# Row blocks 2 to 7 of w3 transposed on VectorE, in a Nystrom attention with a folded feed-forward

## Chip, core and metric

The kernel runs on one core of a Trainium2 chip. A core has five engines with queues of their own, each strictly in order: TensorE (PE, matrix products; PEld is its loading of weights), VectorE (DVE), ScalarE (ACT), GpSimd (POOL) and SyncE (SP), which here only issues transfers. They share an on-chip memory of 128 partitions (SBUF) and an accumulator memory (PSUM) that TensorE writes and VectorE and ScalarE read. 16 DMA engines move data between it and the chip's memory; transfers are issued on the queues of SP, ACT (together "hardware", q1 and q10 in the profile) and POOL ("software", q0, which can also change the type). The metric is the device time of one execution in microseconds (us), as the median of the runs shown.

## What is computed

Inputs: q, k, v of shape (8 batches, 8 heads, 576 rows, 64), and weights w1, w2 (512 x 1024), w3 (1024 x 1024), w_out (1024 x 512), all f32.

```python
q_lm = q.reshape(B, H, m, S // m, D).mean(axis=3)      # m = 32 landmarks, S = 576
k_lm = k.reshape(B, H, m, S // m, D).mean(axis=3)
A, Bm, C = sm(q, k_lm), sm(q_lm, k_lm), sm(q_lm, k)    # softmax of scaled products
Z = Bm^T / (norm1(Bm) * norminf(Bm) + 1e-6)
for _ in range(6):
    Z = 2 * Z - Z @ Bm @ Z
x = (A @ Z @ C @ v), heads side by side                # (4608, 512)
out = ((x @ w1) * (x @ w2)) @ w3 @ w_out               # (4608, 512)
```

## The kernel before

**Folding the weights.** w3 @ w_out doesn't depend on the data, so the kernel multiplies these two first, into `w34` (1024 x 512, f16 in SBUF). w3 is handled in eight row blocks j of 128 rows. A product on TensorE sums over partitions, so a row block has to be turned: its 1024 columns must lie along the partitions. `turn(j, cc)` (L514) does that for one half cc of 512 columns: four transposes of 128x128 on TensorE (L517) into a PSUM tile `big`, then a split of the result, scaled by 256, into two f16 parts, the high one by ScalarE (L522) and the rest by VectorE (L523); both are kept in `w3t`, four tiles of it. `split(c)` (L508) makes the same two parts of a block of 128 rows of w_out (L510, L511). `product(j, c)` (L526) adds three products of 128x512 (high x high, high x low, low x high; L530) into one PSUM tile; after c = 7 ScalarE writes the row block to `w34` (L533). In all 8 x 8 x 3 = 192 products and 16 turns.

**The loads.** w3 goes through three f32 buffers `w3f`, w_out through six `wof`. `load_w3` (L570) issues a row block as one transfer on SP of 128 rows of 4 KB (blocks 0 and 1 in two halves). q and k come through POOL's queue (L107), which changes them to f16, into two buffers `qkn`; the first of these transfers stands behind a copy on POOL (`gate`, L603) that waits until w_out's piece 4 has landed, so the first weights come ahead of q and k. `paced_w3` (L617) holds row block 4 back in the same way until batch 0's k is there.

**Attention.** For each batch VectorE transposes q and k in blocks of 32x32 (L143), landmarks are sums of rows (`landmarks`, L206 to L216; VectorE for batch 0, POOL for the others), `exchange` moves halves of them between partitions (L219; by TensorE for batches 0 and 1, by transfers for the others), then scores A, B, C (`scores_a`, `scores_b`, `scores_c`), the inverse (`norms`, `squares`, six steps of `inverse`), `values`, `denominators`, `normalise` and `landmark_values`.

**Feed-forward.** `project` (L430) makes, for a batch, g = (Z C v) w1 and the same with w2; `up(j, w)` (L451) multiplies A's normalised rows with g: four products of 288 columns each (L455), ScalarE copies the one for w1 (L459), VectorE multiplies it with the one for w2 (L461) into `ab`. `down(n, half)` (L470) multiplies 128 rows of `ab` with `w34` (L495), ScalarE copies the result (L499) and SP stores it (L502). 64 `up` pairs and 36 `down` of eight products.

**The order.** The text `ORDER` is the program's order: a list of words, each of which emits one step (F the next step of the fold, TK and TQ transposes of k and q, SK and SQ landmarks, E, B, C, A and so on, U for `up`, W for `down`). A word emits all its instructions on all engines at that place, so the queues of all engines follow one list. All of the fold's steps are emitted ahead of the first `up`, because `ab` takes the memory of the fold's pool (L668 to L673). Queues run ahead of one another as far as waits allow.

Of the kernel before, what the change touches and what calls it, by code (L numbers as in the profile page):

```python
# [29 lines left out]
CHAINS = ((0,), (1, 2), (3, 4), (5, 6), (7,))  # L30

ORDER = """
F F F F F F F F F F F F F TK0.0 F F F F F TQ0.0 TQ1.0 F F L3.3 F TK1.0 F F F F F SK0.0 SK1.0 F F
SQ0.0 P.4 F F F F L3.5 F L3.7 F F TQ0.1 TK0.1 SQ1.0 F F L3.6 TK1.1 F E.0 F B.0 F C0.0 SK0.1 N.0
F F F A0.0 R.0 FV.0 TQ1.1 F SK1.1 F I0.0 F F D.0 I1.0 F I2.0 Y0.0 Y1.0 SQ0.1 Y2.0 LK0.2 F X.0 F
I3.0 LK1.2 F F F I4.0 V0.0 V1.0 SQ1.1 LQ0.2 LQ1.2 E.1 F LK0.3 TK0.2 TK1.2 F LK1.3 I5.0 F V2.0
LV0.2 F TQ0.2 TQ1.2 A0.1 Z.0 SK0.2 LV0.1 LV1.1 F M0.0 LV2.1 F LV3.1 D.1 Y0.1 Y1.1 Y2.1 G0.0 G1.0
G2.0 M1.0 SK1.2 F SQ0.2 TK0.3 G3.0 TK1.3 C0.1 X.1 F F F F U0a.0 U0b.0 U1a.0 U1b.0 U2a.0 U2b.0
LQ0.3 TQ0.3 LQ1.3 LK0.4 U3a.0 LV1.2 V0.1 U3b.0 SQ1.2 E.2 U4a.0 U4b.0 B.1 U5a.0 U5b.0 N.1 V1.1
SK0.3 V2.1 R.1 U6a.0 U6b.0 TQ1.3 U7a.0 I0.1 M0.1 LK1.4 LQ0.4 U7b.0 W0.0 SK1.3 I1.1 W1.0 I2.1  # L40
A0.2 LV2.2 TK0.4 LV3.2 W0.1 I3.1 TK1.4 W1.1 I4.1 M1.1 LQ1.4 W0.2 TQ0.4 I5.1 W1.2 SQ0.3 SQ1.3
TQ1.4 Z.1 SK0.4 E.3 SK1.4 SQ0.4 LV0.3 C0.2 G0.1 D.2 G1.1 G2.1 W0.3 Y0.2 G3.1 V0.2 V1.2 Y1.2 V2.2
LV0.4 Y2.2 U0a.1 U0b.1 LV1.3 LK0.5 U1a.1 U1b.1 LV1.4 LK1.5 X.2 U2a.1 U2b.1 U3a.1 U3b.1 Z.2 SQ1.4
E.4 U4a.1 U4b.1 U5a.1 G0.2 TK0.5 U5b.1 U6a.1 U6b.1 M0.2 LQ0.5 LQ1.5 W1.3 U7a.1 LV2.3 U7b.1 LV3.3
M1.2 W0.4 G1.2 G2.2 G3.2 B.3 TK1.5 W1.4 U0a.2 A0.3 W0.5 U0b.2 U1a.2 LV2.4 D.3 Y0.3 Y1.3 SK0.5
U1b.2 Y2.3 C0.3 W1.5 LK0.6 U2a.2 U2b.2 U3a.2 W0.6 X.3 U3b.2 U4a.2 N.3 SK1.5 V0.3 V1.3 V2.3 R.3
U4b.2 TK0.6 W1.6 LV3.4 U5a.2 U5b.2 W0.7 TQ0.5 U6a.2 I0.3 M0.3 LK1.6 TQ1.5 W1.7 I1.3 SQ0.5 LQ0.6
U6b.2 W0.8 I2.3 W1.8 I3.3 U7a.2 U7b.2 W0.9 I4.3 M1.3 W1.9 I5.3 A0.4 LQ1.6 Z.3 C0.4 W0.10 G0.3
G1.3 G2.3 D.4 W1.10 Y0.4 LV0.5 SQ1.5 G3.3 E.5 LV1.5 U0a.3 U0b.3 Y1.4 W0.11 TK1.6 Y2.4 U1a.3
U1b.3 U2a.3 U2b.3 LK0.7 X.4 TK0.7 W1.11 TQ0.6 U3a.3 U3b.3 U4a.3 V0.4 V1.4 V2.4 SK0.6 SK1.6 A0.5  # L50
TQ1.6 W0.12 U4b.3 LV2.5 U5a.3 LV3.5 LK1.7 SQ0.6 U5b.3 Z.4 U6a.3 U6b.3 LV0.6 LV1.6 U7a.3 U7b.3
W1.12 M0.4 M1.4 G0.4 W0.13 SQ1.6 E.6 TK1.7 G1.4 G2.4 G3.4 SK0.7 W1.13 D.5 Y0.5 LQ0.7 Y1.5 Y2.5
C0.5 U0a.4 X.5 W0.14 SK1.7 W1.14 U0b.4 U1a.4 U1b.4 B.5 V0.5 V1.5 V2.5 U2a.4 U2b.4 N.5 W0.15
U3a.4 U3b.4 W1.15 A0.6 TQ0.7 R.5 M0.5 W0.16 U4a.4 I0.5 U4b.4 U5a.4 I1.5 U5b.4 U6a.4 I2.5 LV0.7
LQ1.7 TQ1.7 SQ0.7 SQ1.7 W1.16 I3.5 U6b.4 U7a.4 I4.5 M1.5 U7b.4 I5.5 LV2.6 LV1.7 LV3.6 W0.17 Z.5
C0.6 E.7 W1.17 D.6 G0.5 G1.5 G2.5 W0.18 Y0.6 Y1.6 G3.5 Y2.6 U0a.5 U0b.5 X.6 W1.18 U1a.5 U1b.5
U2a.5 B.7 V0.6 V1.6 V2.6 U2b.5 U3a.5 N.7 U3b.5 W0.19 U4a.5 U4b.5 U5a.5 U5b.5 Z.6 U6a.5 W1.19
LV2.7 G0.6 G1.6 G2.6 LV3.7 R.7 W0.20 A0.7 I0.7 W1.20 U6b.5 M0.6 M1.6 W0.21 U7a.5 G3.6 D.7 I1.7
U7b.5 W1.21 U0a.6 U0b.6 Y0.7 U1a.6 Y1.7 U1b.6 W0.22 W1.22 C0.7 U2a.6 W0.23 U2b.6 U3a.6 Y2.7
U3b.6 W1.23 V0.7 V1.7 V2.7 X.7 I2.7 U4a.6 W0.24 U4b.6 I3.7 U5a.6 W1.24 I4.7 U5b.6 U6a.6 I5.7  # L60
W0.25 Z.7 U6b.6 W1.25 M0.7 M1.7 G0.7 W0.26 U7a.6 U7b.6 W1.26 G1.7 G2.7 G3.7 W0.27 U0a.7 U0b.7
W1.27 U1a.7 U1b.7 W0.28 U2a.7 U2b.7 W1.28 U3a.7 U3b.7 U4a.7 W0.29 W1.29 U4b.7 U5a.7 U5b.7 W0.30
U6a.7 U6b.7 U7a.7 W1.30 U7b.7 W0.31 W1.31 W0.32 W1.32 W0.33 W1.33 W0.34 W1.34 W0.35 W1.35
# [4 lines left out]
def kernel(  # L68
# [93 lines left out]
    def constants():  # L162

        mask4 = consts.tile([128, 4, 32], FP32, name="mask4")
        eye = consts.tile([128, 2, 32], FP32, name="eye")
        onesq = consts.tile([128, 2, 4, 2, 4], FP16, name="onesq")
        nc.vector.memset(mask4, 0.0)
        nc.vector.memset(onesq, 0.0)
        for h in range(4):
            sl = slice(32 * h, 32 * h + 32)  # L170
            nc.vector.memset(mask4[sl, h, :], 1.0)
            for qd in range(2):
                nc.vector.tensor_copy(out=eye[sl, qd, :], in_=ident[sl, sl])
                nc.vector.memset(onesq[sl, qd, :, qd, h:h + 1], 1.0 / X64)

        selc = consts.tile([128, 2, 4, 128], FP16, name="selc")
        lomask = consts.tile([128, 1], FP32, name="lomask")
        selr = consts.tile([128, 8], FP32, name="selr")
        nc.vector.memset(selc, 0.0)
        nc.vector.tensor_tensor(out=selr, in0=eye[:, 0, 0:8], in1=eye[:, 0, 8:16], op=ALU.add)  # L180
        nc.vector.reduce_sum(out=lomask, in_=eye[:, 0, 8:16], axis=AX.X)
        nc.vector.tensor_scalar(out=lomask, in0=lomask, scalar1=-1.0, scalar2=None, op0=ALU.mult)
        for c in range(4):
            sl = slice(32 * c, 32 * c + 32)
            for qd in range(2):
                nc.vector.tensor_copy(
                    out=selc[sl, qd, c, :].rearrange("p (h m) -> p h m", m=32),
                    in_=selr[sl, 4 * qd:4 * qd + 4].unsqueeze(2).to_broadcast([32, 4, 32]),
                )
        eye2 = consts.tile([128, 32], FP32, name="eye2")  # L190
        nc.vector.tensor_tensor(out=eye2, in0=eye[:, 0], in1=eye[:, 0], op=ALU.add)
        bt = consts.tile([128, 4, 64], FP32, name="bt")
        for i in range(4):
            nc.vector.tensor_copy(out=bt[:, i, 32:64], in_=eye[:, 0])
        xsp = [consts.tile([128, 256], FP32, name=f"xsp{i}") for i in range(2)]
        for t in xsp:
            nc.vector.memset(t, 0.0)
        return mask4, eye, eye2, onesq, selc, lomask, bt, xsp


# [18 lines left out]
    def exchange(st):  # L219
        if st["b"] < 2:  # L220
            psE = big()
            for x in range(2):
                nc.tensor.matmul(psE[:, 0, 256 * x:256 * x + 256], pick[:, x, :],
                                 st["lm"][:, :, x].rearrange("p t l c e -> p t (l c e)"),
                                 start=True, stop=True)
            nc.scalar.copy(out=st["lm"].rearrange("p t x l c e -> p x t (l c e)"),
                           in_=psE[:, 0, :].rearrange("p (x t f) -> p x t f", x=2, t=2))
            return
# [104 lines left out]
    def values(st, n):  # L333
        if n == 0:
            st["psV"] = big()
# [169 lines left out]
    def fold(pf, wof, w3f, wsp, warm_up):  # L505
# [39 lines left out]
        for n, (j, c) in enumerate(order):  # L545
            for f, *args in before.get(n, ()):
                f(*args)
# [158 lines left out]
```

## Time and profile before

| what | value |
|---|---|
| median of 3 runs | 264.17 us (264.1 to 264.42) |
| span of the profiled execution, first to last instruction | 261.8 us |
| TensorE busy | 251.5 us, 96% |
| VectorE busy | 173.8 us, 66% |
| ScalarE busy | 134.7 us, 51% |
| GpSimd busy | 103.2 us, 39% |
| transposes of w3 on TensorE (L517) | 64, first at 4.6 us, last at 57.0 us |
| low halves of w3 on VectorE (L523) | 16, 687 ns each |
| DMA: bytes moved, mean rate | 37.78 MB, 144 GB/s |

One execution was recorded; its span is 2.4 us less than the median of the timed runs, which are other executions and have what lies around the span in them. In rows of the profile "line engine operation, out<-in xcount | busy us, mean ns of one | idle us before, what ended it" the tiles go by the program's names, and L517 is line 517 of the code above. TensorE's products overlap, so a row's mean duration is longer than the distance from one to the next.

### The profile page before, as it was taken

Reading aid. Unit: us, or ns where it says so; the run is one execution under the profiler, and the core shown is the slowest. Engines: PE = TensorE matmul, PEld = TensorE weight load, DVE = VectorE, ACT = ScalarE, POOL = GpSimd, SP = SyncE. Lnnn points to the kernel's source line nnn. Section 1 sums busy time; section 2 is a strip of 40 time slices with the busy share of each in tenths; the row PEclk is TensorE's granted clock in tenths of the full one; section 3 lists DMA queues with packets and bytes.
Section 4 is the critical chain, followed back from the end, with each engine's and each line's share of the span. In section 5 each row is a group of like instructions: output and inputs, shape, how many; then the busy total and the mean of one; then the engine's idle time right before and its main releaser. Section 6 shows DMA issues by size and latency. Waiting matters only on the chain.

```text
span 261.8 us, 10518 instructions
## 1 busy us (share of the span) xinstructions
PE 251.5 (96%) x4578; PEld 148.7 (57%) x4578; DVE 173.8 (66%) x352; ACT 134.7 (51%) x305; POOL 103.2 (39%) x134
## 2 busy tenths in 40 slices
PE   7999999998989999999999999999999999999993
PEld 3455554454556558557654674766476556656642
DVE  8765887556958687788856958767775656464410
ACT  4543236343652565576449546746646555455531
POOL 3630018998981999027092597504400000000000
PEclk9999999999999999999999999999999999999999
DMA  6999998999963448976668496933640713222355
GB/s 236 333 243 284 245 248 191 183 137 240 175 105 50 120 101 167 216 195 114 131 100 162 101 214 150 161 58 86 147 86 3 173 43 80 45 62 61 81 118 127
DMA packets 25070, 37.78 MB, mean 144 GB/s; under 512 B 4672, under 2 KB 13120, under 8 KB 25024
## 3 DMA queue, kind: packets, MB, share of 16 engines
q1 hardware_dynamic: 14704, 24.65, 36.9%
q0 software_dynamic: 9728, 11.54, 28.1%
q10 hardware_dynamic: 592, 0.92, 1.1%
q8 instruction: 36, 0.59, 1.0%
q14 instruction: 10, 0.08, 0.1%
HBM read 38.80 MB, written 9.44 MB: 184 GB/s over the span
## 4 chain that ended last, share of the span: by engine, by line
PE 89%; DVE 4%; ACT 3%; issue 1%; DMA 1%; SPq 0%; DVEq 0%; ACTq 0%
PE big L455 23%; PE acc L495 22%; PE acc L530 14%; PE big L442 5%; PE big L344 5%; PE big L399 4%; PE big L517 2%; PE small L530 2%; PE big L382 2%; PE small L421 2%; PE big L274 1%; PE big L495 1%; PE big L322 1%; DVE ab L461 1%; PE small L248 1%
## 5 line engine op out<-in xcount | busy, mean ns | idle before, releaser
L455 PE MATMUL big<-ahat,gt 128*128 128x288 f16 x512 | 73.1, 287 | 0.7 <-DVE ab L461 0.6
L495 PE MATMUL acc<-w,ab 128*128 128x512 f16 x264 | 67.2, 380 | 0.0
L461 DVE TENSOR_TENSOR ab<-a_sb,big 128x576 f16<-128x576 f16 x64 | 48.0, 750 | 27.2 <-ACT a_sb L459 16.8
L455 PEld LDWEIGHTS <-gt 128*128 128x128 f16 x512 | 48.3, 98 | 21.1 <-issue 3.1
L459 ACT CAST a_sb<-big 128x576 f16<-128x576 f32 x64 | 40.8, 640 | 33.9 <-PE big L455 32.9
L206 POOL TENSOR_TENSOR tr<-qkT 128x1024 f32<-128x1024 f16 x14 | 29.7, 2123 | 70.0 <-DVE qkT L143 69.8
L530 PE MATMUL acc<-wsp,w3t 128*128 128x512 f16 x168 | 41.3, 380 | 0.7 <-ACT w L533 0.5
L495 PEld LDWEIGHTS <-ab 128*128 128x128 f16 x280 | 25.3, 98 | 24.9 <-issue 3.5
L499 ACT ACTIVATE o_sb<-acc 128x512 f32<-128x512 f32 x33 | 19.8, 599 | 19.5 <-PE acc L495 19.1
L530 PEld LDWEIGHTS <-w3t 128*128 128x128 f16 x192 | 18.1, 98 | 18.9 <-issue 1.3
L143 DVE STREAM_TRANSPOSE qkT<-qkn 128x576 uint32<-128x576 uint32 x32 | 24.0, 763 | 2.0 <-DMA qkn<-in_k_dram 2.0
L448 DVE TENSOR_SCALAR gt<-big 128x1024 f16<-128x1024 f32 x16 | 19.1, 1211 | 3.1 <-PE big L442 3.0
L446 ACT ACTIVATE gt<-big 128x1024 f16<-128x1024 f32 x16 | 15.9, 1032 | 5.9 <-PE big L442 5.9
L211 POOL TENSOR_TENSOR tr<-tr 128x512 f32<-128x512 f32 x14 | 17.9, 1282 | 0.6
L442 PE MATMUL big<-wup,zt 64*32 64x512 f16 x512 | 17.4, 380 | 0.2 <-ACT en L282 0.2
L523 DVE SCALAR_TENSOR_TENSOR w3t<-big,w3t 128x512 f16<-128x512 f32 x16 | 11.0, 687 | 10.0 <-ACT w3t L522 10.0
L522 ACT ACTIVATE w3t<-big 128x512 f16<-128x512 f32 x16 | 9.5, 596 | 13.9 <-PE big L517 13.8
L284 DVE STREAM_TRANSPOSE ent<-en 128x576 f32<-128x576 f32 x16 | 12.1, 768 | 4.4 <-ACT en L282 4.4
L344 PE MATMUL big<-vt,ent 64*32 64x64 f32 x1152 | 14.2, 226 | 0.0
L282 ACT ACTIVATE en<-big 128x288 f32<-128x288 f32 x32 | 12.7, 411 | 2.9 <-PE big L274 2.7
L344 PEld LDWEIGHTS big<-vt,ent 64*32 64x32 f32 x1152 | 12.7, 105 | 2.0 <-ACT a_sb L459 0.5
L328 ACT ACTIVATE eat<-big 128x576 f16<-128x576 f32 x16 | 9.6, 652 | 7.3 <-PE big L322 7.3
(214 smaller groups left out, 285.2 us busy)
## 6 DMA issues: line engine op xcount, KB each, us to landing
out_dram<-o_sb SPq DMA_DIRECT2D x70, 128.0 KB, 2.5
vt<-in_v_dram SPq DMA_DIRECT2D x16, 288.0 KB, 5.3
vt<-in_v_dram SPq DMA_DIRECT2D x32, 144.0 KB, 4.0
qkn<-in_k_dram POOLq DMA_DIRECT2D x12, 288.0 KB, 5.4
qkn<-in_q_dram POOLq DMA_DIRECT2D x12, 288.0 KB, 4.9
w3f<-in_moe_w_dram SPq DMA_DIRECT2D x6, 512.0 KB, 6.7
wup<-in_moe_w_dram POOLq DMA_DIRECT2D x4, 512.0 KB, 25.3
wof<-in_moe_w_out_dram SPq DMA_DIRECT2D x6, 256.0 KB, 4.5
```

The lines of the kernel that those rows point to most:

```text
L143: nc.vector.transpose(out=st["qkT"][:, t, prs].rearrange("p c r q e -> p (c r q e)").bitcast(U32), in_=st["qkn"][:, t, prs, :].rearrange(" ...
L206: add(out=tr, in0=x[:, :, 0:4, :], in1=x[:, :, 4:8, :], op=ALU.add)
L211: add(out=tr[:, :, 0:2, :], in0=tr[:, :, 0:2, :], in1=tr[:, :, 2:4, :], op=ALU.add)
L344: nc.tensor.matmul(psV[32 * o:32 * o + 32, qd, 0:64], ent[sl, pr, r, :], vt[sl, pr, 64 * r:64 * r + 64], start=(r == 0), stop=(r == RT - 1 ...
L442: nc.tensor.matmul(psG[o:o + 32, qd, :], zt[rs, i, h, :], wup[rs, h, w, fs], start=(i == 0), stop=(i == 1), tile_position=(64 * qd, o))
L448: nc.vector.tensor_scalar(out=g[:, :, w, fs], in0=psG, scalar1=1.0 / ZS, scalar2=None, op0=ALU.mult)
L455: nc.tensor.matmul(p[:, c, 0:HS], st["g"][:, qd, w, 128 * j:128 * j + 128], st["ahat", qd][:, c, :], start=(qd == 0), stop=(qd == 1))
L459: nc.scalar.copy(out=st["a_sb"], in_=p[:, :, 0:HS])
L461: nc.vector.tensor_tensor(out=st["ab"][:, j, st["t0"]:st["t0"] + S].rearrange("p (c s) -> p c s", c=2), in0=st["a_sb"], in1=p[:, :, 0:HS], ...
L495: nc.tensor.matmul(pso[:, :], ab[:, j, t0:t0 + 128], w34[:, j, :], start=(j == 0), stop=(j == 7))
L499: nc.scalar.activation(out=o_sb, in_=pso, func=AXF.Copy, scale=1.0 / (X64 * X64))
L530: nc.tensor.matmul(psW[j][:, :], turned[j, c // 4][:, a, c % 4, :], wsp[:, b, c, :], start=(c == 0 and a + b == 0), stop=(c == 7 and a == 1))
```

## The change

Row blocks 0 and 1 of w3 are still turned by TensorE. Row blocks 2 to 7 are turned by VectorE's transpose, which turns each block of 32x32 by itself. To make that a whole turn, the row block is loaded with its four groups of 32 rows and 128 columns laid out so that only turns inside 32 partitions are left: partition 32a + r holds, for each of four row groups g, 128 neighbouring columns of row 32g + r. That takes eight transfers a row block, each of 32 x 4 pieces of 128 columns (512 B), in place of one. The transpose reads every fourth column; so the columns of w3 that lie along the partitions are taken in steps of four, and w_out's rows are loaded in the same steps, and so are the columns that TensorE's transposes read. The turned block goes to a tile `en`, which the scores C use too (two buffers in SBUF), and is split from there.

```diff
+NPE = 2
...
     def load_w3(j, cc=None, eng=nc.sync):
...
-        sl = slice(0, DF) if cc is None else slice(512 * cc, 512 * cc + 512)
-        eng.dma_start(out=w3f[j][:, sl], in_=moe_w3[128 * j:128 * (j + 1), sl])
+        src = moe_w3[128 * j:128 * j + 128, :]
+        if j < NPE:
+            sl = slice(0, DF) if cc is None else slice(512 * cc, 512 * cc + 512)
+            eng.dma_start(out=w3f[j][:, sl], in_=src[:, sl])
+        else:
+            for x in range(2):
+                for a in range(4):
+                    eng.dma_start(
+                        out=w3f[j][32 * a:32 * a + 32, 512 * x:512 * x + 512].rearrange("r (g f) -> r g f", g=4),
+                        in_=src.rearrange("(g r) (x a f) -> x a r g f", g=4, x=2, a=4)[x, a])
...
-        eng.dma_start(out=wof[c], in_=moe_w_out[128 * c:128 * c + 128, :])
+        eng.dma_start(out=wof[c], in_=moe_w_out.rearrange("(x m c) o -> x c m o", x=2, c=4)[c // 4, c % 4])
...
+    def turned_w3(j, cc):
+        if j < NPE:
+            wt = big()[:, 0, :]
+            src = w3f[j].rearrange("p (x m c) -> p x c m", x=2, c=4)
+            for c in range(4):
+                nc.tensor.transpose(out=wt[:, 128 * c:128 * c + 128], in_=src[:, cc, c], identity=ident[:, :])
+        else:
+            wt = pat.tile([128, 2, RT * 32], FP32, name="en").rearrange("p c f -> p (c f)")[:, 0:512]
+            src = w3f[j].rearrange("p (x g i c) -> p x c g i", x=2, g=4, c=4)
+            nc.vector.transpose(out=wt.rearrange("p (c g r) -> p c g r", c=4, g=4), in_=src[:, cc])
+        yield
+        w3t = w3ts[j, cc] = pf.tile([128, 2, 4, 128], FP16, name="w3t", bufs=4)
+        hi, lo = (w3t[:, i].rearrange("p c j -> p (c j)") for i in range(2))
+        nc.scalar.activation(out=hi, in_=wt, func=AXF.Copy, scale=WS)
+        yield
+        nc.vector.scalar_tensor_tensor(out=lo, in0=wt, scalar=WS, in1=hi,
+                                       op0=ALU.mult, op1=ALU.subtract)
```

The second part: every step becomes a generator that yields between its parts on different engines, and `ORDER` (now some 1,500 words) names a step once for each of its parts. So the parts of one step no longer stand together in the list: its part on VectorE can come behind other steps' parts for TensorE. `up` for instance:

```diff
-    def up(st, j, w):
-        p = big()
+    def up(st, j):
+        for w in range(2):
+            p = big()
...
+            yield
+            if w == 0:
+                a_sb = po.tile([128, 2, HS], FP16, name="a_sb", bufs=2)
+                nc.scalar.copy(out=a_sb, in_=p[:, :, 0:HS])
+                yield
+        nc.vector.tensor_tensor(...)
...
+    pab, live = [], {}
+    for word in ORDER.split():
+        if word not in live:
+            if word[0] == "U":
...
+            work = started(word)
+            if word == "K":
+                continue
+            live[word] = work
+        if live[word] is not None:
+            next(live[word], None)
```

In the new `ORDER` (S is `split`, Tx.j half x of row block j, F.j one step of row block j's product, KC the constants, LF the first loads behind the gate, LK and LQ loads of halves of k and q, L loads of w3):

```diff
+K K K KC KC T0.0 KC T0.0 T0.0 S.0 K S.0 K LO.6 K S.1 K K K KC K S.1 K T0.1 T0.1 LK1.2 T0.1 F.0 S.2
+S.2 F.0 LO.7 L.2 LK0.2 F.1 F.1 KC S.3 T1.0 S.3 KC L.3 T1.0 S.4 S.5 F.1 F.0 T1.1 T1.0 F.0 KC LF S.6
...
+TK1.0 F.2 F.2 T1.2 F.2 T0.3 P.4 T1.2 KC F.2 TK0.0 F.2 L.6 F.2 F.2 LQ1.2 F.2 T1.3 T0.3 F.1 TQ1.0 F.2
```

Both halves of batch 2's k (LK1.2, LK0.2) now stand ahead of LF, so POOL issues them before the gate; batch 2's q halves are issued between the first loads of batches 0 and 1. Batches 0 and 2 hold the two `qkn` buffers, so batch 1's k and q are loaded once batch 0's are transposed, and w1 and w2 behind them on POOL's queue (before: directly behind batch 0's and 1's loads). The row blocks are loaded in the order 2, 3, 4, 6, 5, 7 (before: 2, 3, 4, 5, 7, 6).

## The prediction

> **What bounds the kernel now.** I read the page first (busy shares, chain), then the table by stages, the groups of TensorE and VectorE, the chain around one turn, and the DMA view.
>
> ```profile
> PE 251.5 (96%) x4578; PEld 148.7 (57%) x4578; DVE 173.8 (66%) x352; ACT 134.7 (51%) x305; POOL 103.2 (39%) x134
> ...
> PE 89%; DVE 4%; ACT 3%; issue 1%; DMA 1%; SPq 0%; DVEq 0%; ACTq 0%
> ...
> 0.00:17.50 17.50, 15.79 (x72) 7.57 (x73) 12.45 (x54) 8.34 (x14) 8.51 (x24) 1.00 0.93 278
> 17.50:37.60 20.10, 19.60 (x106) 10.59 (x105) 15.16 (x26) 6.13 (x11) 0.18 (x1) 1.00 1.14 255
> 37.60:69.50 31.90, 30.32 (x611) 15.73 (x609) 20.55 (x45) 15.99 (x44) 28.02 (x33) 1.00 1.01 192
> 69.50:99.10 29.60, 27.63 (x820) 17.59 (x819) 22.40 (x44) 15.05 (x38) 22.50 (x26) 1.00 0.51 97
> 99.10:254.00 154.90, 154.56 (x2959) 95.08 (x2956) 102.83 (x186) 87.66 (x195) 44.02 (x52) 1.00 0.55 115
> ```
>
> The last five rows are stretches: length, then busy time of PE, PEld, DVE, ACT, POOL, granted clock (full everywhere), DMA share, GB/s. TensorE sets the end: from 99.1 us to its last product it is idle 0.3 us, in 69.5 to 99.1 2.0 us, before that 3.8 us (1.2 at the start, 1.3 one stall at 58.6 that nothing in the profile explains). 69.5 is where the first `up` product (L455) starts; all turning of w3 lies before it. So the change acts in the first 69.5 us, where the DMA engines are full as well (share 0.93 to 1.14) and VectorE has holes (21 us idle of 69.5).
>
> ```profile
> 22.95 0.44 PE big L517 x4
> 23.39 1.96 PE acc L530 x9
> ...
> 25.37 0.60 ACT w L533
> ...
> L517 PE MATMUL big<-ident,w3f 128*128 128x128 f32 x64 | 10.0, 280 | 0.3 <-DMA w3f<-in_moe_w_dram 0.3
> ...
> L523 DVE SCALAR_TENSOR_TENSOR w3t<-big,w3t 128x512 f16<-128x512 f32 x16 | 11.0, 687 | 10.0 <-ACT w3t L522 10.0
> ...
> L284 DVE STREAM_TRANSPOSE ent<-en 128x576 f32<-128x576 f32 x16 | 12.1, 768 | 4.4 <-ACT en L282 4.4
> ```
>
> The first three are pieces of the chain (start, length): a turn of four blocks holds the chain for 0.44 us though one transpose is shown as 280 ns, since they overlap. VectorE's 10.0 us of waiting ahead of L523 is for ScalarE's half of the split, which itself waits for the turn.
>
> **The change, part by part.**
>
> *TensorE loses 12 of 16 turns* (48 of 64 transposes; the built program's list has exactly 48 fewer): 12 x 0.44 = 5.3 us. Every other product is there in the same number, the 12 warm-up products too.
>
> *VectorE gains 12 transposes* of 128x512 f32. Rows: 768 ns for 576 columns (L284), 285 for 128 (L262), so 1.08 ns a column and about 0.70 us each: 8.4 us. The source is read with a stride of four elements; bound: L216, which also reads with a stride, takes 290 ns for 128 columns, and L355, which doesn't, 291. So nothing to 10% more; I take nothing. ScalarE and the second half read SBUF instead of PSUM: L510 and L511 do that in 622 and 676 ns against 596 and 687; no cost.
>
> Adding up every queue of the built program up to the first `up` product with these rows' durations (products by their spacing on the chain, 0.216 us for 512 columns): TensorE 62.3 us before, 57.0 after; VectorE (to its first L461) 54.5 before, 62.3 after; ScalarE 31 in both. VectorE becomes the longer queue of the front. Rows overlap a little (its 54.5 is about 49 of busy time), so it's about even with TensorE, and what decides is what it waits for, in order.
>
> *The loads of w3.* Each of six row blocks was one DMA of 128 packets of 4 KB (issue 0.33 us); it is now eight DMAs, 1024 packets of 512 B: 48 issues, 15.8 us on SP. SP is idle then, but each of its DMAs waits for the eighth one before it to land, so a block follows another only as that lands. Price of a packet:
>
> ```profile
> q1 hardware_dynamic: 430, 0.78, 103.5%
> ...
> q1 hardware_dynamic: 251, 0.90, 60.4%
> q0 software_dynamic: 309, 0.34, 49.2%
> ...
> q0 software_dynamic: 548, 0.61, 120.2%
> ```
>
> Queue, packets, MB, share of 16 engines: at 8 to 10 us alone, at 22 to 26 with POOL's queue q0, and q0 alone at 18 to 21. 2 KB packets take 77 ns (103.5% x 32 us / 430), 4 KB ones 154: no fixed part, so 512 B would be 22 ns. Bounds: 15 ns (the exchange at 70 to 73 us, 216 packets of about 190 B in 6.8% of 48 us) and 77 ns. I take 22, being on the line through both rows. With both queues full they take turns packet by packet (251 to 309). At one 22 ns packet to each of q0's (about 90 ns, 1.15 KB), w3 moves 73 KB/us, against 225 before (0.90 MB in 4 us).
>
> *POOL's queue.* Batch 2's k (0.59 MB) is now loaded ahead of the gate on wof[4], issued at 3.2 us where POOL's constants end; 2.7 us later (issue 9.5, first packets at 12.2 in this trace) it shares the engines with the first weights, and takes 2.9 us of them (0.205 MB/us). So wof[4] lands at 11.8 instead of 9.0, batch 0's q and k start at 15.0 instead of 12.2, and its q lands at about 22.5 (21.0). The first products need each wof piece at about that time; I count 1.3 us of stall to the end of blocks 0 and 1. The two turns that are gone there (0.9 us) hide most of it.
>
> *The chain through VectorE*, row by row: w3[2]'s first half lands at 15.2, right behind the wof pieces; from 15.0 on q0 is full, so its second half (0.26 MB at 73 KB/us) takes until 18.6 and w3[3]'s first until 22.2, landing at 22.6. VectorE's turn of w3[3] stands ahead of batch 0's first transpose and of the low half of w3[2], for which TensorE's fifth step of block 2 waits: TensorE stands there some 4 us. From 22.6 VectorE has 15.5 us of work (four turns, four low halves, four qkn transposes, landmarks 6.5 us) and 0.5 of waiting until batch 0's landmarks are done: 38.3. With bytes shared evenly it would be 36. Before, the exchange that needs them (L223) ran at 37.6, with three more product steps (1.9 us) and five turns still to come. From there TensorE needs 31.9 - 2.7 (five turns: 2 x 0.44, 3 x 0.59 on the chain) + 1.9 - 2.8 (its waits before) = 28.3 us, VectorE about 28, both in order and tied to one another (inverse, values, denominators): 2 us of waits on top. First `up`: 36 + 30.3 = 66.3 to 38.3 + 30.3 = 68.6, against 69.5; I take 67.5, the middle.
>
> *The order behind that* moves the same instructions: TensorE has 170.5 us by the same rows in both, VectorE and ScalarE the same. There is 2.3 us of idle time to win and nothing else; I take 0. The tail from the last product on (last copy waits for all stores) is unchanged.
>
> *Sum.* 261.8 - 2.0 = 259.8 for the span; the median of the runs is 264.17, 2.4 more than the profiled span, so 262.2.
>
> **The rivals.**
>
> Full gain: shares are kinder than packet by packet, VectorE is never late, TensorE keeps its idle 3.8 us: first `up` at 57.0 + 7.2 = 64.2 us; 264.17 - 5.3 = 258.9. For it: VectorE's 21 us of holes. Against: 8.4 us of turns and the q and k of batch 0 later by 1.5 us.
>
> Slower, by starved loads: packets of 512 B cost what 2 KB ones do (77 ns). w3 then moves 45 KB/us beside q0: w3[3]'s halves land at 27 and 32.5 instead of 22.6 and 26.1, everything on VectorE behind them is 6 us later, and the first `up` comes at 67.5 + 6 = 73.5: 264.17 + 4.0 = 268.2. It decides from about 35 ns a packet (2 us, by the same proportion). Or, with cheap packets, if a queue's turn is several of them: the counts of 251 to 309 fit turns of any equal length, but a new DMA holds only 8 packets for each engine (128 over 16; 0.18 us), and against 12 of q0's, say (1.1 us), 64 KB come in 1.28 us, 50 KB/us, nearly the same rate and the same time. For both: full engines, queues in order. Against: the straight line through two sizes, and that no row shows turns of many. [...]
>
> Slower or same, by the new order: TensorE was idle 0.3 us after 99.1, so each hole of the new order is a loss: 0.5 to 1 us of waits in each of the four pairs of batches takes the 2.0 back and up to 2 more, 264 to 266. For it: nothing of the old slack is in reserve; against: products of two `up` steps are interleaved, and between scores and norms of batches 1 and 2 now stand 4.7 us of other products where TensorE had waited 1.0 us.
>
> That the turns stay is excluded by the built list.
>
> **How the numbers follow.** Forecast 45% (260.5 to 264.3; its upper end is no change), full gain 14%, starved loads 28% (16 by dear packets, 12 by long turns), new order 13%. 0.2% (0.5 us) is about what a measurement of this kernel tells from no change. Faster: 40 + 14 = 54%; same: 5 of the forecast, 5 of the order = 10%; slower: 28 + 8 = 36%. Range 258.3 to 267.5: it leaves out the worse half of the starved loads and a little below.
>
> **What would show it.** First `up` at 66 to 69 us; TensorE with a wait of some 4 us for a low half of w3t near 21 us and one of 1 to 3 us at the exchange; VectorE's transposes 0.70 us; w3 packets 22 ns, landing 3 to 8 us after issue; PE idle after 99 us under 2 us. Wrong if the transposes take over 1 us, if the first `up` is past 70, or if the gain or loss lies behind it.

## The result, and the profile after

The changed kernel takes 300.45 us (median of 4 runs, 297.99 to 302.55); beside it the kernel before took 264.3 us. The ratio is 1.132, 95% interval 1.124 to 1.141: 13% slower, against a forecast of 262.2 us. Like every ratio and every median in the table below, this ratio leaves out executions that took over 1.5% longer than the fastest of their kernel. The profiled execution has a span of 296.9 us (before 261.8).

From here on "front" is the time from the start to the first `up` product, "body" the time from there to the last one. Before: front 69.5, body 179.1 us. After: front 88.9, body 194.1. So 19.4 us were lost ahead of the first `up`, 15.0 behind it, and 0.7 in the tail.

The page of the changed kernel: busy times, TensorE's row of slices and its granted clock (9 stands for full speed, 5 for half), TensorE's instruction queue (packets, MB, share of the DMA engines), and the chain of waits by engine.

```profile
PE 258.0 (87%) x4530; PEld 149.3 (50%) x4530; DVE 187.7 (63%) x364; ACT 133.9 (45%) x305; POOL 103.9 (35%) x134
...
PE   5966987644999699999989969969998999899994
...
PEclk9995999955999899999999986997999999999999
...
q8 instruction: 35, 0.57, 0.9%
...
PE 69%; DMA 9%; issue 6%; DVE 3%; ACT 1%; SPq 1%; DVEq 0%; ACTq 0%
```

TensorE lost 48 products (x4530, before x4578) and is busy for longer: 258.0 us, before 251.5. Its share of the chain fell from 89% to 69%; DMA took 9%, and "issue", time in which nothing that the profile shows is waited for, 6%. The clock row has gaps of half speed; before it was full throughout.

The stretches that answer to those of the prediction (length, busy PE, PEld, DVE, ACT, POOL, granted clock, DMA share, GB/s), cut at the start of the exchange and at the first `up` of this kernel:

```profile
0.00:17.50 17.50, 14.27 (x60) 7.29 (x61) 10.35 (x42) 8.02 (x14) 6.30 (x21) 1.00 0.97 257
17.50:43.40 25.90, 19.47 (x78) 7.84 (x76) 19.66 (x33) 5.83 (x10) 5.05 (x9) 0.87 0.91 174
43.40:88.90 45.50, 32.94 (x598) 16.14 (x599) 33.77 (x61) 16.14 (x44) 27.18 (x30) 0.85 0.84 164
88.90:117.90 29.00, 25.81 (x644) 16.16 (x643) 19.81 (x41) 14.44 (x39) 21.83 (x25) 0.94 0.63 117
117.90:289.00 171.10, 161.66 (x3131) 99.55 (x3130) 103.69 (x189) 87.71 (x196) 43.55 (x51) 0.97 0.44 97
```

The exchange comes at 43.4 us (37.6 before, 38.3 predicted), and from there to the first `up` it takes 45.5 us instead of 31.9. In the last row TensorE is idle 9.4 us, where before it was idle 0.3 us.

What TensorE waited for (us in total, times, longest), and two groups of VectorE:

```profile
PE big L396 <- issue: 4.7, 2, 3.8
PE big L337 <- DMA vt<-in_v_dram: 4.7, 3, 2.2
PE big L337 <- issue: 4.6, 3, 2.5
PE acc L544 <- DVE w3t L537: 4.3, 2, 3.0
PE big L343 <- issue: 2.8, 1, 2.8
PE small L298 <- issue: 2.6, 1, 2.6
```
```profile
L531 DVE STREAM_TRANSPOSE en<-w3f 128x512 f32<-128x512 f32 x12 | 12.9, 1083 | 6.7 <-DMA w3f<-in_moe_w_dram 6.7
L537 DVE SCALAR_TENSOR_TENSOR w3t<-en,w3t 128x512 f16<-128x512 f32 x12 | 10.0, 836 | 0.5 <-ACT w3t L535 0.5
```

The four issue rows are 14.7 us in seven stalls (before: one of 1.3 us). The transpose takes 1083 ns, not the 700 predicted, and VectorE waits 6.7 us for pieces of w3.

The loss in one sum, up to the last `up` product: TensorE's idle time grew from 6.1 to 34.9 us (28.8 more), its busy time from 242.5 to 248.1 (5.6 more). As its products were to take 5.3 us less, I estimate that the lower clock cost about 10.9 us. 28.8 + 5.6 = 34.4 us, which is 19.4 + 15.0.

### The profile page after: what moved, and what is told of

The parts are those of the page before. It is cut to its first block, busy times and chain, and to the rows that moved or that the text cites. A ratio compares the mean times of both kernels' runs of the same rounds, so it can differ in the third digit from the quotient of the medians.

```text
span 296.9 us, 10457 instructions
## 1 busy us (share of the span) xinstructions
PE 258.0 (87%) x4530; PEld 149.3 (50%) x4530; DVE 187.7 (63%) x364; ACT 133.9 (45%) x305; POOL 103.9 (35%) x134
## 4 chain that ended last, share of the span: by engine, by line
PE 69%; DMA 9%; issue 6%; DVE 3%; ACT 1%; SPq 1%; DVEq 0%; ACTq 0%
PE big L460 22%; PE acc L502 20%; DMA w3f<-in_moe_w_dram 7%; PE big L445 5%; PE big L337 5%; PE acc L544 4%; PE big L396 3%; DMA vt<-in_v_dram 3%; PE small L422 1%; PE big L502 1%; PE big L378 1%; PE big L261 1%; PE big L316 1%; DVE en L531 1%; PE small L298 1%
## 5 line engine op out<-in xcount | busy, mean ns | idle before, releaser
L460 PE MATMUL big<-ahat,gt 128*128 128x288 f16 x512 | 77.0, 296 | 0.1
L502 PE MATMUL acc<-w,ab 128*128 128x512 f16 x264 | 68.8, 386 | 0.1
L460 PEld LDWEIGHTS <-gt 128*128 128x128 f16 x512 | 49.9, 101 | 22.8 <-issue 3.1
L544 PE MATMUL acc<-wsp,w3t 128*128 128x512 f16 x168 | 43.3, 405 | 4.6 <-DVE w3t L537 4.3
L337 PE MATMUL big<-vt,ent 64*32 64x64 f32 x1152 | 15.9, 236 | 9.3 <-DMA vt<-in_v_dram 4.7
L452 DVE TENSOR_SCALAR gt<-big 128x1024 f16<-128x1024 f32 x16 | 19.4, 1215 | 4.4 <-PE big L445 4.1
L337 PEld LDWEIGHTS big<-vt,ent 64*32 64x32 f32 x1152 | 13.9, 110 | 11.4 <-issue 5.1
L130 POOL DMA_DIRECT2D qkn<-in_k_dram x14 | 10.4, 746 | 24.9 <-DVE qkT L166 24.6
L450 ACT ACTIVATE gt<-big 128x1024 f16<-128x1024 f32 x16 | 15.7, 1021 | 6.0 <-PE big L445 5.9
L531 DVE STREAM_TRANSPOSE en<-w3f 128x512 f32<-128x512 f32 x12 | 12.9, 1083 | 6.7 <-DMA w3f<-in_moe_w_dram 6.7
L535 ACT ACTIVATE w3t<-en 128x512 f16<-128x512 f32 x12 | 7.4, 628 | 17.9 <-DVE en L531 17.9
L382 DVE TENSOR_TENSOR ahat<-eat,big 128x576 f16<-128x576 f16 x16 | 12.0, 749 | 5.3 <-PE big L378 5.3
```

What stands on the lines that cost most here:

```text
L337: nc.tensor.matmul(psV[32 * o:32 * o + 32, qd, 0:64], ent[sl, pr, r, :], vt[sl, pr, 64 * r:64 * r + 64], start=(r == 0), stop=(r == RT - 1 ...
L452: nc.vector.tensor_scalar(out=g[:, :, w, fs], in0=psG, scalar1=1.0 / ZS, scalar2=None, op0=ALU.mult)
L460: nc.tensor.matmul(p[:, c, 0:HS], st["g"][:, qd, w, 128 * j:128 * j + 128], st["ahat", qd][:, c, :], start=(qd == 0), stop=(qd == 1))
L502: nc.tensor.matmul(pso[:, :], ab[:, j, t0:t0 + 128], w34[:, j, :], start=(j == 0), stop=(j == 7))
L544: nc.tensor.matmul(psW, w3ts[j, c // 4][:, a, c % 4, :], wsp[:, b, c, :], start=(c == 0 and a + b == 0), stop=(c == 7 and a == 1))
```

## The experiments

All kernels at a glance: median of the runs, ratio to the kernel before on the same chip with its interval, and from the profiled execution front, body and TensorE's issue stalls. The kernels ran on several chips, so differences of time between them are taken from their ratios here (0.01 is 2.64 us). The profiled executions of new_order_pe_turns and old_order_dve_turns took 3.7 and 5.2 us longer than the medians listed; their fronts and bodies are too long by that in sum.

| kernel | us | ratio | front | body | issue |
|---|---|---|---|---|---|
| before | 264.17 | | 69.5 | 179.1 | 1.3 |
| changed | 298.68 | 1.132 (1.124 to 1.141) | 88.9 | 194.1 | 14.7 |
| new_order_pe_turns | 276.91 | 1.047 (1.038 to 1.056) | 79.3 | 185.3 | 6.4 |
| old_order_dve_turns | 292.74 | 1.105 (1.094 to 1.116) | 85.0 | 198.1 | 14.1 |
| new_front_old_body | 298.93 | 1.132 (1.122 to 1.141) | 90.1 | 192.9 | 12.7 |
| old_front_new_body_pe_turns | 274.15 | 1.036 (1.028 to 1.043) | 69.5 | 187.7 | 6.2 |
| before_80_tiny | 277.24 | 1.049 (1.043 to 1.056) | 72.8 | 190.7 | 7.9 |
| old_order_dve_turns_48_tiny | 280.21 | 1.062 (1.056 to 1.068) | 84.8 | 181.1 | 1.0 |
| after_48_tiny | 282.95 | 1.071 (1.068 to 1.074) | 83.1 | 182.9 | 4.6 |
| after_whole_blocks | 285.17 | 1.079 (1.076 to 1.082) | 77.4 | 191.6 | 12.7 |
| after_48_late_k | 291.04 | 1.098 (1.092 to 1.103) | 89.9 | 186.4 | 5.5 |
| after_48_contiguous_turns | 284.06 | 1.071 (1.067 to 1.076) | 82.8 | 185.6 | 6.1 |
| old_order_last_2_turned | 269.76 | 1.022 (1.017 to 1.026) | 74.2 | 179.4 | 1.1 |
| old_order_last_3_turned | 277.80 | 1.051 (1.048 to 1.055) | 77.6 | 185.1 | 3.1 |
| after_48_whole | 277.57 | 1.050 (1.045 to 1.056) | 74.6 | 184.8 | 8.0 |
| after_48_sixteen_rows | 282.24 | 1.070 (1.064 to 1.075) | 82.6 | 184.8 | 8.1 |
| old_48_whole | 275.75 | 1.044 (1.039 to 1.048) | 82.1 | 179.1 | 1.6 |
| old_48_whole_contiguous | 274.13 | 1.038 (1.032 to 1.043) | 79.4 | 179.1 | 1.8 |
| before_one_product | 263.95 | 0.998 (0.995 to 1.000) | 69.5 | 179.3 | 0.4 |
| before_two_products | 263.19 | 0.996 (0.994 to 0.999) | 70.4 | 179.4 | 0 |

### Order or turns?

The steps of the changed kernel can be put in any order (its `ORDER` has 1,091 words, not some 1,500), so the old ORDER was written in the new words (an F word as one call of `F.j`, preceded by the S and T steps that the old `fold` placed there, and so on). With all turns on TensorE this gives the instruction lists of the kernel before on every engine, only the columns of w3 and rows of w_out paired in fours. Four kernels cross the two parts:

```diff
# new_order_pe_turns: the new ORDER
-NPE = 2
+NPE = 8
# old_order_dve_turns: NPE = 2, ORDER = the old one, step for step
# new_front_old_body: ORDER = new up to the first U0.0, then what is left in the old order
# old_front_new_body_pe_turns: NPE = 8, ORDER = old up to the first U0.0, then what is left in the new order
```

> The changed kernel's order, with all eight row blocks of w3 turned by TensorE and loaded whole (one DMA of 4 KB rows each) instead of the 48 pieces; the order of all steps stays. Theory 'starved' (the 48 pieces and the dear transposes cost the front 19.4 us, and the stalls behind the front follow from that): first product of up for batch 0 near 69-73 us, total 264-272 us. Theory 'two costs' (19.4 us at the front from the loads and turns, and 14.4 us behind it from the order of the body alone): first product of up near 69-73 us, total 278-286 us. Theory 'order' (the new order does it all): first product of up past 84 us, total 295-305 us.

> The order of the kernel before, step for step on every engine, with blocks 2 to 7 turned by VectorE and loaded in 48 pieces. 'Starved' and 'two costs': the pieces are issued in the old places, so the front still loses 12-20 us (first product of up at 81-89 us) and the body loses nothing, total 276-285 us. 'Order': first product of up within 2 us of 69.5, total 262-267 us.

> The changed kernel word for word up to its first product of up, and from there the words left over in the old order. 'Two costs': first product of up at 89 us as in the changed kernel, and the 14.4 us behind it come back: total 284-288 us. 'Starved' (the stalls behind the front follow from the late front): 296-303 us.

> The old order and TensorE turns up to the first product of up, and from there the words left over in the new order. 'Two costs': first product of up at 69-70 us, total 276-281 us, with the issue stalls of TensorE (0.9 to 3.8 us each) still there behind 95 us. 'Starved': 262-268 us, and no issue stall behind 95 us.

No theory held in all four: of the totals only that of new_front_old_body lies in a range (that of "starved"), while "two costs" has the fronts of the last three about right. The order alone costs 4.7%, the turns alone 10.5%, which adds up to more than the 13.2% of the whole change. The old body behind the new front brings nothing back (ratio 1.132, that of the changed kernel), while the new body behind the old front costs 9 us. And old_order_dve_turns, whose body has exactly the instructions of the kernel before in the same order, takes 198.1 us for it instead of 179.1, of which at most 5 us are that long execution's own. What differs there is what lies ahead: the front is later, and 48 products and 48 weight loads of TensorE, 96 instructions, are gone.

### Where the instruction packets are cut

TensorE's instructions come through a DMA queue of their own: 35 packets, 0.57 MB, so 16 KB each, and 9,060 products and weight loads make some 259 instructions a packet; I take 256: from the first of the stalls below to the last 7,424 instructions pass, 29 times 256. I counted TensorE's instructions in the trace (products, weight loads and waits on semaphores) against the starts of these packets, with the place of packet n taken as 256 n behind the earliest start. For the seven stalls of the changed kernel (us):

```
line  begins  length  instructions past the packet's place  packet's start to the end of the stall
L396    67.0    3.78                 277                          2.53
L298    99.0    2.55                 277                          2.33
L396   151.6    0.91                 277                          2.26
L343   174.2    2.84                 277                          2.89
L337   197.7    2.50                 277                          2.48
L337   227.7    0.93                 277                          2.45
L337   254.5    1.19                 277                          2.72
```

Each begins at the same count (to within one instruction), and ends 2.3 to 2.9 us after a packet's start. In the other kernels, too, all issue stalls over 0.3 us of one kernel begin at one count. The same burst shows both ways. In the changed kernel (timeline: start, length, idle time before in brackets):

```profile
170.19 2.12 PE L460 MATMUL big<-ahat,gt 128*128 128x288 f16 x16
172.24 1.85 PE L337 MATMUL big<-vt,ent 64*32 64x64 f32 x140
...
176.99 0.31 PE L343 MATMUL big<-sums,eye 64*32 64x1 f32 x14 [2.84 <-issue]
177.22 0.74 PE L316 MATMUL big<-qkT,lm 32*32 32x288 f16 x32
...
179.58 3.93 PE L460 MATMUL big<-ahat,gt 128*128 128x288 f16 x16
```

The values are 144 products with 144 weight loads in 1.7 us: more than a packet, in less than the 2.2 us that pass at least from a packet's start to the end of a stall. Behind the stall the same 16 `up` products take 3.93 us instead of 2.12, at half the clock. To move the cuts and nothing else, tiny products (32x1) were put at TensorE's start (80 take 2.30 us), 80 into the kernel before (160 instructions; 256 - 160 = 96, as if 96 were gone) and 48 into the others (the 96 back):

```diff
# before_80_tiny
     warm_up(7)
+    for _ in range(80):
+        nc.tensor.matmul(psw[0:32, 0, 0:1], warm[:, 0:32], warm[:, 0:1], start=True, stop=True)
# old_order_dve_turns_48_tiny and after_48_tiny: the same with range(48), behind the 7th and 3rd warm-up product
```

> The kernel before with 80 tiny products (32x1, with their weight loads 160 instructions) ahead of TensorE's first turn and nothing else: the instruction stream of TensorE behind them is shifted by 160, which stands to its packets of 256 instructions as the 96 instructions taken out by the turns do. Theory 'phase' (what was lost behind the front with the old order and VectorE turns is the place at which the 256-instruction packets cut the bursts of small products): body from the first to the last product of up 188-199 us instead of 179, with 'issue' stalls of 1.2 to 2.9 us in the sums and squares as in that run; total 275-287 us. Rival 'late front' (the stalls come from transfers that a late front pushes into the body): body 178-181 us, total 264-268 us.

> Old order, blocks 2 to 7 turned by VectorE, and 48 tiny products (96 instructions) at the start, as many as the 48 transposes that left TensorE. 'Phase': the front stays late (first product of up 83-88 us), the body is back at 178-183 us and its issue stalls of over 1 us are gone; total 276-283 us. 'Late front': 293-298 us with the same stalls.

> The changed kernel and 48 tiny products (96 instructions) at the start. 'Phase': the body goes from 194 us to what the new order with TensorE turns had, 184-187 us, the front stays at 86-91 us; total 288-293 us. 'Late front': 297-302 us.

"Phase" held three times, though the gain in after_48_tiny is larger than it forecast (282.95 us against 288 to 293, front 83.1 against 86 to 91). The 80 tiny products cost the unchanged kernel 13 us (4.9%; in the profiled execution 14.9, 11.6 of it in the body); the 48 give old_order_dve_turns 11 us back (ratio 1.105 to 1.062), nearly all of it in the body; and they make the changed kernel 16 us faster (1.132 to 1.071; by the profiled executions 17.0, 5.8 in the front and 11.2 in the body). That the same act costs one kernel time and saves it in two others speaks against a rival cause at the start, such as a later start of TensorE's work. In after_48_tiny the burst of above goes through without a stop:

```profile
165.07 2.12 PE L460 MATMUL big<-ahat,gt 128*128 128x288 f16 x16
167.13 1.84 PE L337 MATMUL big<-vt,ent 64*32 64x64 f32 x140
...
169.02 0.54 PE L316 MATMUL big<-qkT,lm 32*32 32x288 f16 x32
169.49 1.04 PE L502 MATMUL acc<-w,ab 128*128 128x512 f16 x4
170.36 1.88 PE L460 MATMUL big<-ahat,gt 128*128 128x288 f16 x14
```

Two kernels meant as better versions, with only the last blocks turned by VectorE, give doses between (32 and 48 instructions fewer):

```diff
# old_order_last_2_turned and old_order_last_3_turned: the old ORDER, T steps of the blocks from NPE on
# moved to six (cc = 0) and three (cc = 1) products ahead of their block
-NPE = 2
+NPE = 6
# and 5
```

> The old order, with only blocks 6 and 7 of w3 turned by VectorE (16 pieces) and their turns three to six products ahead of their use; 32 instructions fewer on TensorE. 'Phase' by the rows of the trace before: a packet boundary moved by 32 meets no burst, body 178-181 us; the front saves 4 turns of 0.44 us: total 261.5-263.5 us. Rival 'pieces' (SP's 16 issues of 0.43 us instead of 2 hold batch 0's v): first product of up 71-75 us, total 266-270 us.

> The same with blocks 5, 6 and 7 (24 pieces); 48 instructions fewer on TensorE. 'Phase': body 178-182 us, the front saves 6 turns of 0.44 us: total 260.5-263.5 us. Rival 'pieces': first product of up 73-78 us, total 268-273 us.

With 32 fewer the body is as before (179.4 us), with 48 fewer 185.1 us with stalls of 1.14, 0.50 and 1.11 us: the "phase" forecast of no harm was too kind for 48. Both totals miss the range of "phase" (261.5 to 263.5 and 260.5 to 263.5 us) above all because the fronts are late. These (74.2 and 77.6 us) lie in the range of the rival "pieces", though not by its cause in the first: there TensorE waits three times 1.6 to 1.9 us for the first batch's inverse, whose steps on VectorE and ScalarE now stand behind turns.

### The loads

```diff
# after_whole_blocks (new order), after_48_whole (and the 48 tiny products)
-            for x in range(2):
-                for a in range(4):
-                    eng.dma_start(
...
+            eng.dma_start(out=w3f[j], in_=src)
# after_48_sixteen_rows
+            for i in range(8):
+                eng.dma_start(out=w3f[j][16 * i:16 * i + 16, :], in_=src[16 * i:16 * i + 16, :])
# after_48_late_k: ORDER with the four loads of batch 2 behind the last LF, LF 5 and 6 right behind LF 4
```

> The changed kernel with blocks 2 to 7 of w3 loaded whole, one DMA of 4 KB rows each, and turned in the same 32x32 blocks: the blocks then stand in other places of w3's transpose, so the last factor is another matrix; the work of every engine is the same. Theory 'pieces' (SP's 48 issues and the landing of 512 B packets hold the front): first product of up at 73-80 us, total 284-292 us, since the body keeps its stalls. Rival 'turns' (VectorE's 1.08 us transposes and the order hold the front): first product of up at 85-89 us, total 295-301 us.

> The changed kernel with the 48 tiny products and whole loads of blocks 2 to 7 (the blocks then stand in other places of w3's transpose, the last factor is another matrix). Theory 'they add' (11.5 us of the pieces and 5.8 us of the packet boundary are two costs): first product of up 70-74 us, total 266-271 us. Rival 'they share': first product of up 75-79 us, total 271-277 us.

> As after_48_whole, but each block in 8 DMAs of 16 whole rows: 48 DMAs of 64 KB as in the changed kernel, in packets of 4 KB. Theory 'packets' (the 512 B packets cost): first product of up within 2 us of after_48_whole. Theory 'issues' (SP's 48 issues cost): within 2 us of the 83.1 us of after_48_tiny.

> The changed kernel with the 48 tiny products, and GpSimd's loads back in the old order: the q and k of batches 0 and 1 and the weights first, the four loads of batch 2 behind them. Theory 'early batch 2' (its loads ahead of the gate delay wof[4], batch 0's q and batch 1's k): first product of up at 79-82 us instead of 83.1, total 279-282 us. Rival 'pieces alone': first product of up within 0.7 us of 83.1, total 282-284 us.

With whole loads, and with those of sixteen whole rows, the turned blocks stand in other places of w3's transpose, so these kernels compute another last factor; the counts of instructions are the same. Whole loads bring the first `up` from 88.9 to 77.4 us, with the tiny products from 83.1 to 74.6. So in the front 11.5 and 5.8 us nearly add: 14.3 of 17.3 us. The total of after_48_whole, 277.57 us, lies above both ranges (266 to 271 and 271 to 277): its body is 1.9 us longer than that of after_48_tiny, with 8.0 us of issue stalls in all instead of 4.6. SP's part of it, in the timeline of the changed kernel and then of after_48_whole:

```profile
9.34 37.38 SPq L579 DMA_DIRECT2D w3f<-in_moe_w_dram  x48
48.12 2.23 SPq L149 DMA_DIRECT2D vt<-in_v_dram  x2
```
```profile
9.61 22.80 SPq L577 DMA_DIRECT2D w3f<-in_moe_w_dram  x6
32.50 1.45 SPq L149 DMA_DIRECT2D vt<-in_v_dram  x2
```

The loads of batch 0's v stand behind w3's on SP and go out at 48.1 instead of 32.5 us; the three waits for vt (4.7 us) are gone with whole loads. Why eight DMAs a block are slower is told only in part. Sixteen rows each came in packets of 2 KB (1004 packets, 2.07 MB on SP's queue at 15 to 35 us), not of 4 KB as expected, and cost as much as the 512 B pieces (front 82.6). In that stretch an engine moves 14.1 bytes in a ns of packet time with the pieces, 13.9 with sixteen rows and 24.3 with whole blocks (from packets, MB and share: 32, 149 and 147 ns a packet). So it isn't the 512 B alone. What both slow forms share is 64 KB DMAs into 32 or 16 partitions each; which of the two counts wasn't tried.

after_48_late_k turned the sign of a term round, and neither theory held: the old order of GpSimd's loads makes the changed kernel 7 us slower (1.071 to 1.098). With it TensorE waits 3.2 us at the exchange (1.7 in after_48_tiny) and 5.3 us at `scores_c` (none), and VectorE 15.7 us for w3 (5.2). Loading batch 2 first keeps batch 1 and the weights w1 and w2 waiting for a free buffer (GpSimd issues them from 35.1 us on in the changed kernel). Between 5 and 45 us GpSimd's queue then moves 3.73 MB instead of 4.51, and SP gets 47 pieces of w3 out instead of 36.

### The turns on VectorE

```diff
# after_48_contiguous_turns; old_48_whole_contiguous has this and the whole loads, old_48_whole the whole loads alone,
# both in the old order with the 48 tiny products
-            src = w3f[j].rearrange("p (x g i c) -> p x c g i", x=2, g=4, c=4)
-            nc.vector.transpose(out=wt.rearrange("p (c g r) -> p c g r", c=4, g=4), in_=src[:, cc])
+            nc.vector.transpose(out=wt, in_=w3f[j][:, 512 * cc:512 * cc + 512])
```

> The changed kernel with the 48 tiny products, whose 12 VectorE transposes read 512 neighbouring columns instead of every fourth one, so that w3's transpose has its rows in another order than w_out's and the last factor is another matrix. Theory 'stride': a transpose takes 0.66-0.74 us instead of 1.08, the waits of TensorE for w3t shrink, first product of up 1-3 us earlier than 83.1, total 279-282 us. Rival 'fp32 block transposes cost that anyway': 1.0-1.1 us each, total 282-284 us.

> The old order with the 48 tiny products, blocks 2 to 7 loaded whole and turned by VectorE (last factor another matrix, as above). Theory 'the turns pay once the loads are whole' (12 turns of 0.44 us leave TensorE): first product of up 65-69 us, total 259-264 us. Rival 'VectorE is late' (1.08 us transposes stand ahead of the chain of the first batch on VectorE): first product of up 70-76 us, total 265-272 us.

> As old_48_whole, with transposes that read neighbouring columns (0.70 us instead of 1.08). 'The turns pay': first product of up 64-68 us, total 258-263 us. 'VectorE is late': 1-3 us earlier than old_48_whole and still past 69 us, total 263-269 us.

The stride is the whole difference in price (with neighbouring columns the last factor is again another matrix). The group of after_48_contiguous_turns (busy us, mean ns):

```profile
L530 DVE STREAM_TRANSPOSE en<-w3f 128x512 f32<-128x512 f32 x12 | 8.3, 697 | 10.2 <-DMA w3f<-in_moe_w_dram 10.2
```

But the 4.6 us that VectorE saves are spent waiting for w3 (10.2 us instead of the 5.2 of after_48_tiny), and the time stays (284.06 against 282.95 us, the intervals overlap). In the old order the turns don't pay even with whole loads: "VectorE is late" held, and by more than it expected (front 82.1 us, 79.4 without the stride). Timeline of old_48_whole, TensorE and then VectorE:

```profile
27.74 5.69 PE L543 MATMUL acc<-wsp,w3t 128*128 128x512 f16 x24 [1.06 <-ACT w L546]
37.86 7.65 PE L543 MATMUL acc<-wsp,w3t 128*128 128x512 f16 x21 [4.43 <-ACT w L546]
```
```profile
30.95 1.22 DVE L189 TENSOR_TENSOR tr<-qkT 128x1024 f32<-128x1024 f16 x1
...
34.38 1.23 DVE L189 TENSOR_TENSOR tr<-qkT 128x1024 f32<-128x1024 f16 x1
35.53 1.07 DVE L530 STREAM_TRANSPOSE en<-w3f 128x512 f32<-128x512 f32 x1
37.35 0.69 DVE L536 SCALAR_TENSOR_TENSOR w3t<-en,w3t 128x512 f16<-128x512 f32 x1 [0.76 <-ACT w3t L534]
```

And ScalarE:

```profile
36.69 0.63 ACT L534 ACTIVATE w3t<-en 128x512 f16<-128x512 f32 x1 [6.38 <-DVE en L530]
37.23 0.58 ACT L546 ACTIVATE w<-acc 128x512 f16<-128x512 f32 x1
```

TensorE waits for ScalarE to read out the block product before (L546; there is one `acc`). That copy stands in ScalarE's queue behind the high half of the next block (L534), which waits 6.38 us for the turn at 35.5 us, and this stands in VectorE's queue behind batch 0's landmarks. The step that cost TensorE 0.44 us now goes through two engines whose queues hold other work, in both directions.

### The one stall of the kernel before

```diff
# before_one_product: one F, before_two_products: two F from behind V2.0 to ahead of it
-... LK1.3 I5.0 F V2.0 LV0.2 F TQ0.2 TQ1.2 A0.1 Z.0 SK0.2 LV0.1 LV1.1 F M0.0 ...
+... LK1.3 I5.0 F F F V2.0 LV0.2 TQ0.2 TQ1.2 A0.1 Z.0 SK0.2 LV0.1 LV1.1 M0.0 ...
```

> The kernel before with one step of block products (three products, 0.65 us) moved from behind the last third of batch 0's values to ahead of it. Theory 'packet': the packet that the sums wait for has 0.65 us more to come, the 1.27 us stall at 58.6 us shrinks to 0.4-0.8 us, total 0.3-0.9 us below before (263.3-263.9 us). Rival 'something else in the sums': the stall stays at 1.1-1.4 us behind the moved step, total within 0.3 us of before.

> The same with two steps (1.30 us) moved. 'Packet': the stall is below 0.3 us, total 0.8-1.5 us below before, unless the landmark values behind it (ahead of the first up) now wait for VectorE. Rival: stall 1.1-1.4 us, total within 0.3 us of before.

"Packet" held for the stall: it goes from 1.27 to 0.42 us to none. Timeline of the kernel before, of before_one_product, then of before_two_products:

```profile
57.15 0.81 PE L530 MATMUL acc<-wsp,w3t 128*128 128x512 f16 x3
57.89 0.67 PE L344 MATMUL big<-vt,ent 64*32 64x64 f32 x44
...
59.89 0.26 PE L349 MATMUL big<-sums,eye 64*32 64x1 f32 x12 [1.27 <-issue]
```

```profile
57.79 1.46 PE L529 MATMUL acc<-wsp,w3t 128*128 128x512 f16 x6
59.18 0.67 PE L343 MATMUL big<-vt,ent 64*32 64x64 f32 x44
...
60.32 0.27 PE L348 MATMUL big<-sums,eye 64*32 64x1 f32 x15 [0.42 <-issue]
```
```profile
58.93 2.10 PE L529 MATMUL acc<-wsp,w3t 128*128 128x512 f16 x9
60.97 0.90 PE L343 MATMUL big<-vt,ent 64*32 64x64 f32 x47
```

before_two_products beats both kernels: 263.19 us against 264.06, ratio 0.9963, interval 0.9938 to 0.9987 (its profiled execution has another wait of 1.6 us at 20 us, for a low half of w3t, and shows nothing of the gain). One step alone can't be told from no change.

## Why the prediction was wrong

All three signs of being wrong that it names came: transposes of 1.08 us, a first `up` at 88.9 us, and a loss behind it, of 15.0 us.

*What bounds the kernel.* TensorE, as said. But "one stall that nothing in the profile explains" was the trace's only sign of what cost most: it is a stall of the same kind as the seven, as the two kernels just shown tell.

*"TensorE loses 12 of 16 turns ... 12 x 0.44 = 5.3 us."* The 48 products are gone. This is the step that failed most: taking 96 instructions out of a list that comes in packets of some 256 was priced as a gain alone, 5.3 us, and it moved the cuts of all packets behind them. Measured by putting 96 back: a loss of 16 us (ratio 1.132 to 1.071).

*"Nothing to 10% more; I take nothing."* The stride of four costs 55% (1083 against 697 ns). The rows chosen for the bound were additions, not transposes; the trace had none of a strided transpose. Its effect on the time can't be seen in the new order, where VectorE then waits for w3; in the old one with whole loads it is 1.6 us (275.75 to 274.13), and the intervals overlap.

*The loads of w3.* The mechanism was right (pieces wait for one another: SP stood 17 times, 12.4 us in all, until an earlier piece, the eighth before, had landed; w3 comes late, TensorE stands for a low half near 21 us: 1.99 and 2.96 us there, 4 predicted). The size was not. 22 ns a packet was 32, close to the 35 from which the rival of starved loads was to decide; block 3's first half was there for VectorE at 27.1 us instead of 22.6, and the exchange came 5.1 us later than forecast. That rival's price (6 us at the first `up`) was too low too, since it followed VectorE's queue alone: v's loads, queued behind w3's on SP, cost 4.7 us more. (By the prediction's own figures its w3 moves 49 KB/us beside q0, not 45, and the chain through VectorE ends at 38.6, not 38.3; both are small beside the misses.) With both queues full, at 16 to 25 us, SP's and GpSimd's moved 1,238 packets each, and w3 came at 62 KB/us (0.56 MB in 9 us), not 73; how many packets a queue's turn has, one as in the forecast or 12 of GpSimd's as in the rival's second case, no run shows. Pieces for whole loads: 8.5 to 11.5 us of front.

*GpSimd's queue.* "1.3 us of stall" by the early loads of batch 2. The gate's copy ran at 9.7 us, not 11.8, and the early loads gain some 7 us in the changed order instead of costing any.

*"The chain through VectorE": first `up` at 67.5.* It came at 88.9. From the exchange on 28.3 us of TensorE and 2 us of waits were counted, and 45.5 us passed, with waits for v (4.7), an issue stall (3.8) and a granted clock of 0.85 among the causes.

*"The order behind that ... I take 0."* The content is the same, as said; the body is 15.0 us longer, 11.2 of them by the cuts. What stays is the new order's own (after_48_tiny 3.8 us, old_front_new_body_pe_turns 8.6): in it, too, issue stalls remain (4.6 and 6.2 us over the whole kernel), as other bursts meet the packets' cuts. The rival of the new order named the place and took 0.5 to 1 us a pair of batches.

*Full gain* had no ground: old_48_whole_contiguous has whole loads, cheap transposes, the cuts as before and 12 turns less on TensorE (its 48 tiny products take 1.4 us, by the 2.30 us of 80), and is 10 us slower than the kernel before.

In sum, of 35 us (the ratio of 1.132): 16 by the packets' cuts (to 1.071), 5.5 by the pieces (to 1.050), and some 13 by the new order with VectorE's turns, 8.0 us of issue stalls at other places (in after_48_whole) among them. Of these 13 the runs tell only that either alone costs time; how they divide stays open.

## What to carry to other kernels

TensorE's instruction list came in packets of some 256. Where TensorE runs more than a packet of small products in a burst (here 288 instructions in 1.7 us, with a stall of 2.84 us behind them), count instructions before a change takes some out, and look at "issue" waits at a fixed distance. A few tiny products at the start moved every cut (80 cost one kernel 13 us, 48 gave two others 11 and 16 us back), and six large products moved ahead of a burst filled a wait of 1.27 us. A transfer cut into pieces was paid by what stood behind it in its queue, here v (issued at 48.1 us instead of 32.5). Work moved to an engine with idle time was late by what stood ahead of it in that engine's queue, though VectorE was busy for only 66% of the span before (ScalarE waited 6.38 us for one turn).

## What the runs showed of the hardware

- TensorE's instructions came in packets of 16 KB (35 in the changed kernel, some 256 instructions each); it stopped some 271 to 295 instructions behind a packet's place (one number, to within one, for all such stalls over 0.3 us of one kernel, 277 in the changed one; it differs between kernels with the earliest start, which sets the places), and went on 2.2 to 2.9 us after the packet's start. Such stalls took 14.7 of the 296.9 us of the changed kernel, four of the seven in the products of a batch's values or right behind them, whose 288 instructions pass in 1.7 us.
- After many of these stalls, and of other waits, the granted clock was half, in stretches of 3.4 us (in the changed kernel from 101.3 and from 200.3 us on), 6.8 (from 22.8 and from 176.4), 13.7 (from 60.4) or 10.2 (in after_48_late_k). Stalls of 1.75 and 2.12 us in old_order_dve_turns were followed by one, those of 2.47 us there and 2.42 us in before_80_tiny (clock 1.00 from 163.1 to 170 us) were not.

```profile
166.00:174.00 8.00, 8.00 (x198) 5.96 (x191) 5.38 (x9) 4.99 (x9) 0.00 (x0) 1.00 0.76 174
177.00:181.00 4.00, 4.00 (x56) 1.96 (x56) 1.15 (x3) 1.41 (x3) 0.00 (x0) 0.50 0.02 4
```

These two stretches of the changed kernel lie ahead of and behind the stall at 174.2 us (the column before the last two is the granted clock).

- VectorE's transpose of 128x512 f32 took 1083 ns with a stride of four elements (changed kernel) and 697 ns without (after_48_contiguous_turns).
